# Turning the second batch's q by DMA instead of on the matrix engine, in a fused attention and feed-forward kernel

## The chip, the cores and the metric

The kernel runs on one core of a Trainium2 chip. The core has a matrix engine (TensorE, PE in the profile; its weight loads are shown as PEld), a vector engine (VectorE, DVE), an activation engine (ScalarE, ACT), a general engine (GpSimd, POOL) and a queue engine (SyncE, SP). Each works through its own list of instructions in order; semaphores tie the lists together. Transfers between the chip's memory and the core's SBUF are issued from SP, ACT or POOL, and carried out by 16 DMA engines. The metric is the device time of one execution in microseconds (us). Times in the trace count from the start of the span.

## The reference

Eight batches of eight heads go through a linear attention without softmax, are normalised per head, and then go through a gated feed-forward layer whose input is normalised per token:

```python
kv = np.einsum('bhsd,bhse->bhde', k, v)          # 64x64 per head
out = np.einsum('bhsd,bhde->bhse', q, kv)
out = out / sqrt(mean(out * out, -1) + 1e-6) * g_norm
x = out.transpose(0, 2, 1, 3).reshape(B * S, H * D)   # 4608 x 512
xn = x / sqrt(mean(x * x, -1) + 1e-6) * rms_g
out = (silu(xn @ w_gate) * (xn @ w_val)) @ w_out      # 512 -> 1536 -> 512
```

There are 576 tokens in a batch (S), 8 heads (H) of 64 (D). Inputs and output are float32; the kernel multiplies in bfloat16 and accumulates in float32.

## The kernel before, in words

**Tiles.** A batch's 576 tokens are cut into a main part of 512 (four chunks of 128, `NC = 4`) and a remainder of 64 (`REM`). The feed-forward layer works in nine groups of 512 tokens: group b is the main part of batch b, and the last group is the eight remainders together (`xr`). For a group, twelve pairs of products make the hidden tiles (`gate_of` with `wg`, `val_of` with `wv`, line 641), then 48 products with `wo` make four output tiles (line 676).

**q, k, v.** For `out = q kv` the matrix engine needs q with the head dimension on the partitions: that is `qTs`, the turned q, two buffers used by batch in turn. Three ways to get it stand in the program. Batch 0 casts q from a float32 stage and turns it on PE against an identity (`qT_mm`). Batches 2 to 7 load q as float32 on SP (`load_q`, line 217), cast it on POOL (batch 2: on ACT) into `main_q`, and turn it by a DMA on SP (`qT_dma`, lines 332 to 336):

```python
def qT_dma(self):
    flat = mains[self.b, 0].rearrange("p c h d -> p (c h d)")
    nc.sync.dma_start_transpose(out=self.qT[:, 0:NC].rearrange(...), in_=flat)
    rem = rems[0][self.b % 2][:REM].rearrange("p h d -> p (h d)")
    return nc.sync.dma_start_transpose(out=self.qT[:, NC, :, 0:REM], in_=rem)
```

Batch 1, the second, has a way of its own: a POOL-issued DMA loads q and casts it on the way to bfloat16, in the order heads, chunks, dimension (`load_cast`, line 187, into `qc`), and PE turns it head by head (`qT_heads`, line 314: 40 products of a 128 x 64 weight with the identity); DVE and ACT copy the results from PSUM into `qTs[1]` (`qT_out`, line 326).

**The order of the work.** The program writes each engine's list by hand. The feed-forward work is a row of slots; `Placer` keeps, for each slot, the small operations of attention that ride on it, and `emit` writes a slot's operations of other engines first, then the slot's own products, then its PE operations. The row that matters here starts when the second half (columns 256 to 511) of group 0 begins: slots 0 to 11 are that half's gate and value products (8 products of 256 columns each), slots 12 to 27 are the 48 products with `wo` of group 0, three to a slot (`slots_b_by_j`), and slot 28 is the first of group 1, which needs batch 1's turned and normalised result (`x`).

**Batch 1's steps** are put into fixed slots by `place_second(P, 9)` (line 588), all offsets counted from slot 9: `turn_q` on PE in slot 5, its copies in slots 6 to 8; the k-by-v products (`kv_mm`, line 273) in slot 9 and their copies in 10; `oT_mm` (line 380, the first reader of the turned q) in slots 11, 11, 12, 13, 14 for the four head pairs and the remainder; squares on ACT (`sqT_`) a slot or two behind; sums of squares (`stat_mm`) in 15; the output in token order (`o_mm`, line 341) in 16 to 19; the scale chain on DVE from 16; scaling in 18 to 22; and the turning of the result (`xT_mm`, line 520) in 20 to 25, with the last copies in 26.

**The queues around it.** POOL's list (lines 768 to 850) issues the loads of the weights, then waits for and casts batch 0's late q, then issues the cast loads of q, v and k of batch 1, the four loads of `w_out` (`load_wo`, line 230), and the k and v of batch 2. SP's list has, ahead of everything in the slots, `load_q(2)` (line 911: 1024 KB and 128 KB of float32 q of batch 2), which a hand-made dependency holds back until the first `w_out` load has landed. Behind it on SP come, in slot order, batch 2's `qT_dma` and the output stores.

Of the kernel before, what the change touches and what calls it, by code (L numbers as in the profile page):

```python
# [11 lines left out]
BF16 = mybir.dt.bfloat16  # L12
# [3 lines left out]
ACT = mybir.ActivationFunctionType  # L16
# [70 lines left out]
def kernel(  # L87
# [12 lines left out]
    nc = tc.nc  # L100
    B, H, S, D = q.shape
# [3 lines left out]
    NC = 4  # L105
    MAIN = 128 * NC
    REM = S - MAIN
    NS = d_model // 128
    NF = d_ff // 128
# [3 lines left out]
    OB = 3  # L113
# [7 lines left out]
    qkv = pool("qkv", 2)  # L121
# [9 lines left out]
    mm1_p = pool("mm1", 3, space=bass.MemoryType.PSUM)  # L131
    o2_p = pool("o2", 2, space=bass.MemoryType.PSUM)
    att_p = pool("att", 3, space=bass.MemoryType.PSUM)


    ident = consts.tile([128, 128], BF16, name="ident")
# [4 lines left out]
    vc, kc = ([consts.tile([128, H, (NC + 1) * D], BF16, name=f"{t}c{n}") for n in range(2)] for t in "vk")  # L141
    sel = consts.tile([128, 2, 2], BF16, name="sel")
    qc = consts.tile([128, H, (NC + 1) * D], BF16, name="qc1")
# [10 lines left out]
    qTs = [consts.tile([128, NC + 1, NS, 128], BF16, name=f"qTs{n}") for n in range(2)]  # L154
    rems = [[consts.tile([128, H, D], BF16, name=f"remq{n}") for n in range(2)]]
# [20 lines left out]
    mains, xs = {}, {}  # L176
# [10 lines left out]
    def load_cast(b, t, heads=None):  # L187
        to = qc if t == 0 else (vc if t == 2 else kc)[b % 2]
        if heads is None:
            return nc.gpsimd.dma_start(  # L190
                out=to[:REM, :, NC * D :], in_=src[t][b, :, MAIN:S, :].rearrange("h p d -> p h d")
            )
        view = src[t][b, :, 0:MAIN, :].rearrange("h (p c) d -> p h (c d)", c=NC)[:, heads[0] : heads[1]]
        return nc.gpsimd.dma_start(out=to[:, heads[0] : heads[1], : NC * D], in_=view)
# [27 lines left out]
    def loads_kv(b):  # L222
        return [lambda t=t, hs=hs: load_cast(b, t, hs) for t in (1, 2) for hs in ((0, H), None)]

    def load_w(n):
        cols = slice(FB0[n] * 128, (FB0[n] + FB[n]) * 128)
        first = nc.gpsimd.dma_start(out=wg[n], in_=moe_w_gate.rearrange("(s p) f -> p s f", p=128)[:, :, cols])
        return first, nc.gpsimd.dma_start(out=wv[n], in_=moe_w_val.rearrange("(s p) f -> p s f", p=128)[:, :, cols])

    def load_wo(n):  # L230
        view = moe_w_out.rearrange("(c p) d -> p c d", p=128)
        return nc.gpsimd.dma_start(out=wo[n], in_=view[:, n * OB : (n + 1) * OB, :])
# [9 lines left out]
    class Att:  # L242
        def __init__(self, b):
            self.b = b
            self.kv, self.qT = kvs[b % 2], qTs[b % 2]
            if b < 2:
                self.qTj = self.qT.rearrange("p c j t -> p (c j t)").rearrange("p (j c t) -> p j c t", j=NS, c=NC + 1)
            else:
                self.qTj = self.qT.rearrange("p c j t -> p j c t")
            self.kv_chunks = range(NC + 1)  # L250
            self.o, self.outa, self.sq = {}, {}, {}
            self.xT = {}
            self.st = None
# [50 lines left out]
        def qT_mm(self, js, chunks, pool=None):  # L304
            qT_ps = (pool or att_p).tile([128, len(js), len(chunks) * 128], BF16, name="o2" if pool else "att")
            for n, j in enumerate(js):
                for i, c in enumerate(chunks):
                    nc.tensor.matmul(
                        qT_ps[:, n, i * 128 : (i + 1) * 128], lhsT=self.pair(0, c, j), rhs=ident, is_transpose=True,
                        start=True, stop=True, skip_group_check=True,  # L310
                    )
            return qT_ps

        def qT_heads(self, js, chunks):
            qT_ps = att_p.tile([128, len(js), len(chunks) * 128], BF16, name="att")
            for n, j in enumerate(js):
                for i, c in enumerate(chunks):
                    for half in range(2):
                        nc.tensor.matmul(  # L319
                            qT_ps[half * D : (half + 1) * D, n, i * 128 : (i + 1) * 128],  # L320
                            lhsT=qc[:, 2 * j + half, c * D : (c + 1) * D], rhs=ident, is_transpose=True,
                            start=True, stop=True, skip_group_check=True,
                        )
            return qT_ps

        def qT_out(self, ps, js, c0, eng):
# [261 lines left out]
    def place_second(P, s):  # L588
        a = Att(1)
        V, A = nc.vector, nc.scalar  # L590
        ps = {}
        pe = lambda at, cost, n, fn: P.at("PE", cost, lambda: ps.__setitem__(n, fn()), s + at)
        dve = lambda at, cost, fn: P.at("DVE", cost, fn, s + at)
        act = lambda at, cost, fn: P.at("ACT", cost, fn, s + at)

        def turn_q():
            for n, (js, chunks) in enumerate(((P0, range(NC)), (P1, range(NC)), (ALL, (NC,)))):
                ps[n] = a.qT_heads(js, chunks)

        P.at("PE", 1.2, turn_q, s - 4)  # L600
        for j in range(2):
            dve(-3 + j, 0.42, lambda j=j: a.qT_out(ps[0][:, j : j + 1], (j,), 0, V))
            act(-3 + j, 0.58, lambda j=j: a.qT_out(ps[1][:, j : j + 1], (2 + j,), 0, A))
        act(-1, 0.58, lambda: a.qT_out(ps[2], ALL, NC, A))
        P.at("PE", 1.14, lambda: a.kv_mm(range(NS)), s)
        dve(1, 0.43, lambda: a.kv_half(0))
        dve(1, 0.43, lambda: a.kv_half(1))

        parts = [((j,), 0, NC) for j in range(NS)] + [(ALL, NC, NC + 1)]
        for n in range(NC + 1):  # L610
            pe((2, 2, 3, 4, 5)[n], 0.25, ("oT", n), lambda n=n: a.oT_mm(*parts[n]))
            act((3, 4, 4, 5, 6)[n], 0.62, lambda n=n: a.sqT_(ps["oT", n], *parts[n]))
        act(6, 1.28, lambda: A.preload_act_table(ACT.Sqrt))
        P.at("PE", 0.64, lambda: a.stat_mm(0, NC + 1), s + 6)
        for n in range(NC + 1):
            P.at("PE", 0.24, lambda n=n: a.o_mm(n, mm1_p if n == 2 else None), s + (7, 7, 8, 9, 10)[n])
        dve(7, 2.2, lambda: a.lead_chain(0, NC + 1, True))
        for c in range(NC + 1):
            dve(9 + c, 0.68, lambda c=c: a.xna_(c, V, a.o[c]))
        for at, js, cs in ((11, P0, (0, 1)), (13, P1, (0, 1)), (14, P0, (2, 3)), (15, P1, (2, 3))):  # L620
            P.at("PE", 0.24, lambda js=js, cs=cs: a.xT_mm(js, cs), s + at)
            for j in js:
                dve(at + 1, 0.3, lambda j=j, cs=cs: a.xT_out(j, cs, V))
        P.at("PE", 0.15, lambda: a.xT_mm(ALL, (NC,)), s + 16)
        dve(17, 0.62, lambda: [a.xT_out(j, (NC,), V) for j in ALL])
        P.floor = s + 18
        return s + 18

# [135 lines left out]
    V, G, A = nc.vector, nc.gpsimd, nc.scalar  # L764
    H0, H1 = (0, 4), (4, 8)
    P0, P1 = (0, 1), (2, 3)
    ALL = range(NS)
# [17 lines left out]
    make_identity(nc, ident)  # L785
    make_identity(nc, identf)
    w_loads = [load_w(n) for n in range(len(FB))]
    G.memset(rems[0][1][REM:], 0.0)
    G.memset(kvs[1], 0.0)
    for tile_ in (kc[0], kc[1], vc[0], vc[1], qc):  # L790
        G.memset(tile_[REM:, :, NC * D :], 0.0)

    def fold(w, s, eng):
# [6 lines left out]
    a = Att(0)  # L800
# [20 lines left out]
    for i, j in enumerate(P1):  # L821
        a.kv_pairs_out(kvb, i, j)
    V.tensor_scalar(
        out=gain, in0=gall[:, 0:NS], scalar1=gcol, scalar2=float(d_model) ** 0.5, op0=OP.mult, op1=OP.mult
# [20 lines left out]
    for t in (0, 2, 1):  # L845
        load_cast(1, t, (0, H))
        load_cast(1, t)
    wo_loads = [load_wo(n) for n in range(NF // OB)]
    for f in loads_kv(2):
        f()  # L850

    half = MAIN // 2
    early = [Slot("half", lambda: gates(0, range(FB[0]), 0, half))]
    for n, w in enumerate(FB):
        js = range(FB0[n], FB0[n] + w)
# [66 lines left out]
    P = Placer(slots, 3)  # L922
# [55 lines left out]
```

## Time and profile before

| | |
|---|---|
| median of 3 runs | 325.04 us (324.96 to 325.22) |
| the profiled execution | 324.99 us |
| its span in the trace | 323.2 us (1.8 us lie around it) |
| granted TensorE clock | 1.00 |
| PE busy | 312.9 us, 97% of the span |
| DVE, ACT, POOL busy | 178.7, 143.1, 89.3 us |
| DMA | 40.49 MB, a mean of 125 GB/s; 190 to 220 GB/s in the first 65 us |
| SP and ACT transfers (hardware queues) / POOL transfers (software queue) | 32.8% / 34.2% of 16 engines' span |

The page's first part gives each engine's busy time; the chain of work that ended last follows the program back from its last instruction, from each wait to what released it; the timeline lists one engine's instructions with the idle time before each and its releaser; the list of transfers gives, for each group of DMA issues, the size and the median time from issue to landing, and can be asked for a stretch of the span. A matmul's duration is a latency: starts of neighbours overlap, so what one costs is read from the distance of starts, or from the chain. On SP and POOL, a row for a DMA is the time the engine spends issuing it, not the transfer.

### The profile page before, as it was taken

To read this page: it belongs to the slowest core of one execution; us is meant where nothing else is said; L and a number is where in the kernel's file an instruction comes from. 1 tells how busy PE (TensorE), PEld (TensorE's weight loads), DVE (VectorE), ACT (ScalarE), POOL (GpSimd) and SP (SyncE) were. 2 spreads that over 40 slices of the span, in tenths; PEclk is the share of its full clock that TensorE was granted. 3 is DMA by queue.
4 is the path that set the end of the run, shared out by engine and by line. 5 is a ranking of instruction groups with operands and counts; after the bars stand their busy time and mean duration, and the time that the engine had idled before them with its cause. 6 is when DMAs were issued, how large, how long until landed. Compare 5 with 4: busy or idle time off the path is not lost.

```text
span 323.2 us, 5403 instructions
## 1 busy us (share of the span) xinstructions
PE 312.9 (97%) x2041; PEld 162.3 (50%) x2062; DVE 178.7 (55%) x394; ACT 143.1 (44%) x266; POOL 89.3 (28%) x110
## 2 busy tenths in 40 slices
PE   5999999999999999999999999999999999999995
PEld 1678866554454445444554445444544444444443
DVE  4658438489938672857185818681778133203411
ACT  1464566485758323832283228422742233223320
POOL 8763420049016600670067005800420000000000
PEclk9999999999999999999999999999999999999999
DMA  8999999949673984499559956896000800040002
GB/s 215 220 200 198 194 223 217 220 139 147 121 199 107 139 163 140 130 124 158 144 148 108 140 150 173 90 139 162 35 1 0 172 32 0 3 108 21 0 34 97
DMA packets 78213, 40.49 MB, mean 125 GB/s; under 512 B 41960, under 2 KB 73708, under 8 KB 78188
## 3 DMA queue, kind: packets, MB, share of 16 engines
q0 software_dynamic: 30672, 14.16, 34.2%
q1 hardware_dynamic: 46032, 25.01, 31.8%
q10 hardware_dynamic: 1484, 0.99, 1.0%
q8 instruction: 16, 0.26, 0.3%
q14 instruction: 9, 0.07, 0.1%
HBM read 37.78 MB, written 9.44 MB: 146 GB/s over the span
## 4 chain that ended last, share of the span: by engine, by line
PE 89%; DMA 5%; ACT 2%; issue 1%; DVE 1%; POOL 0%; SPq 0%; ACTq 0%; POOLq 0%
PE mm L641 55%; PE o L676 26%; DMA rstg<-in_q_dram 3%; DMA remv<-in_v_dram 2%; PE att L341 2%; PE att L273 2%; PE mm L676 1%; PE o L706 1%; ACT sq L367 0%; PE att L520 0%; ACT silu L650 0%; DVE h L659 0%; PE att L319 0%; ACT outa L371 0%; ACT wv L795 0%
## 5 line engine op out<-in xcount | busy, mean ns | idle before, releaser
L659 DVE TENSOR_TENSOR h<-silu,mm 128x512 bf16<-128x512 bf16 (+1 forms) x120 | 75.7, 631 | 82.4 <-PE mm L641 75.9
L650 ACT ACTIVATE silu<-mm 128x512 bf16<-128x512 f32 (+1 forms) x120 | 66.3, 556 | 82.5 <-PE mm L641 73.3
L641 PE MATMUL mm<-x,wv 128*128 128x512 bf16 (+1 forms) x431 | 99.8, 355 | 0.1
L641 PE MATMUL mm<-x,wg 128*128 128x512 bf16 (+1 forms) x419 | 98.5, 358 | 0.2 <-DVE h L659 0.2
L676 PE MATMUL o<-wo,h 128*128 128x512 bf16 x383 | 87.6, 379 | 1.3 <-issue 0.8
L422 POOL TENSOR_TENSOR sq<-sq,g 128x512 bf16<-128x512 bf16 x30 | 34.6, 1155 | 130.8 <-ACT sq L367 130.7
L641 PEld LDWEIGHTS <-wv 128*128 128x128 bf16 x480 | 46.2, 98 | 44.0
L641 PEld LDWEIGHTS <-wg 128*128 128x128 bf16 x468 | 44.7, 98 | 42.9 <-issue 0.6
L676 PEld LDWEIGHTS <-h 128*128 128x128 bf16 x420 | 40.2, 98 | 46.0 <-DVE h L659 0.2
L692 ACT COPY osb<-o 128x512 f32<-128x512 f32 x33 | 19.3, 587 | 69.4 <-PE o L676 69.4
L427 DVE TENSOR_REDUCE st<-sq 128x8 f32<-128x512 bf16 x60 | 38.8, 678 | 1.1 <-ACT sq L367 0.8
L302 DVE CAST kvs<-att 64x256 bf16<-64x256 f32 x14 | 5.9, 422 | 30.3 <-PE att L273 30.2
L367 ACT ACTIVATE sq<-att 128x512 bf16<-128x512 f32 x30 | 17.9, 598 | 2.2 <-PE att L341 2.2
L494 DVE TENSOR_TENSOR xna<-outa,al 128x512 bf16<-128x512 bf16 x30 | 18.7, 682 | 0.0
L371 ACT CAST outa<-att 128x512 bf16<-128x512 f32 x30 | 17.7, 590 | 0.0
L341 PEld LDWEIGHTS <-qTs 128*128 128x128 bf16 x140 | 10.2, 98 | 6.9
L641 PE MATMUL mm<-xr,wg 128*128 128x512 bf16 x47 | 12.3, 379 | 0.1
L641 PE MATMUL mm<-xr,wv 128*128 128x512 bf16 x47 | 12.3, 379 | 0.1
L341 PE MATMUL att<-kvs,qTs 128*128 128x128 bf16 x136 | 12.2, 219 | 0.0
L208 POOL CAST main_q<-stg 128x1024 bf16<-128x1024 f32 (+1 forms) x12 | 11.3, 976 | 0.7 <-DMA stg<-in_q_dram 0.7
L237 PE MATMUL mm<-idle 128*128 128x512 bf16 x26 | 7.5, 452 | 4.0 <-DVE idle L163 4.0
L795 ACT ACTIVATE wv<-wv,gain 128x384 bf16<-128x384 bf16 x16 | 9.2, 611 | 0.5 <-PE mm L641 0.5
(132 smaller groups left out, 174.5 us busy)
## 6 DMA issues: line engine op xcount, KB each, us to landing
out_dram<-osb SPq DMA_DIRECT2D x31, 256.0 KB, 2.6
stg<-in_q_dram SPq DMA_DIRECT2D x6, 1024.0 KB, 7.0
vc<-in_v_dram POOLq DMA_DIRECT2D x7, 512.0 KB, 8.3
kc<-in_k_dram POOLq DMA_DIRECT2D x7, 512.0 KB, 6.1
wg<-in_moe_w_gate_dram POOLq DMA_DIRECT2D x4, 384.0 KB, 15.6
wv<-in_moe_w_val_dram POOLq DMA_DIRECT2D x4, 384.0 KB, 16.8
wo<-in_moe_w_out_dram POOLq DMA_DIRECT2D x4, 384.0 KB, 13.2
out_dram<-osb SPq DMA_DIRECT2D x8, 128.0 KB, 2.3
```

Of the source, the lines that this page charges most:

```text
L208: return copy(out=mains[b, t][:, cs[0] : cs[1], h0:h1, :], in_=staged[b, t].rearrange("p h (c d) -> p c h d", c=NC)[:, cs[0] : cs[1], h0:h ...
L341: nc.tensor.matmul(o[:, 2 * j : 2 * j + 2, :], lhsT=self.qTj[:, j, c, :], rhs=self.kv[:, j, :, :], start=j == 0, stop=j == NS - 1, skip_gr ...
L367: nc.scalar.activation(out=self.sq[c][:, 0], in_=self.o[c], func=ACT.Square)
L371: (eng.tensor_copy if eng else nc.scalar.copy)(out=self.outa[c], in_=self.o[c])
L422: eng.tensor_tensor(out=self.sq[c][:, 1], in0=self.sq[c][:, 0], in1=g2, op=OP.mult)
L427: nc.vector.reduce_sum(out=self.st[:, which, c, :], in_=self.sq[c][:, which], axis=AX.X)
L494: return eng.tensor_tensor(out=self.xna[:, c], in0=src, in1=self.al[:, c, :].to_broadcast([128, H, D]), op=OP.mult)
L641: nc.tensor.matmul(ps[:, : c1 - c0], lhsT=w[n][:, s, jj * 128 : (jj + 1) * 128], rhs=x_of(g, s, c0, c1), start=s == 0, stop=s == NS - 1)
L650: nc.scalar.activation(out=sis[g, j][:, c0:c1], in_=ps, func=ACT.Silu)
L659: nc.vector.tensor_tensor(out=hs[g, j][:, c0:c1], in0=sis[g, j][:, c0:c1], in1=v_ps, op=OP.mult)
L676: nc.tensor.matmul(ps, lhsT=hs[g, j][:, t * 128 : (t + 1) * 128], rhs=wo[j // OB][:, j % OB, :], start=j == 0, stop=j == NF - 1)
L692: (eng.copy if eng is nc.scalar else eng.tensor_copy)(out=o, in_=ps)
```

## The change

Batch 1's q is still loaded by the POOL-issued cast DMA into `qc`, in the order of heads. POOL then copies it into the order of chunks: two copies (four heads each, 128 x 1024) into `mains[1, 0]` and one of the remainder (64 x 512) into `rems[0][1]`. They stand in POOL's list between the second and the third load of `w_out`. SP turns the result with the same `qT_dma` that the later batches use, placed in slot 5. `turn_q` with its 40 products on PE, and its five copies on DVE and ACT, are gone. All of batch 1's steps from `kv_mm` on stand one slot later; the slot in which later work may begin (`P.floor`, 27) is the same. `qTs[1]` takes the layout of the later batches, with chunks outermost, and one of POOL's early memsets is aimed at it, in place of two.

In SP's list the two transposes come directly behind `load_q(2)`. In PE's list batch 1's first `oT_mm` now stands behind the three products of slot 12.

```diff
@@ Att.__init__
-            if b < 2:
+            if b < 1:
                 self.qTj = self.qT.rearrange("p c j t -> p (c j t)").rearrange("p (j c t) -> p j c t", j=NS, c=NC + 1)
...
-        def qT_heads(self, js, chunks):
-            qT_ps = att_p.tile([128, len(js), len(chunks) * 128], BF16, name="att")
-            for n, j in enumerate(js):
-                for i, c in enumerate(chunks):
-                    for half in range(2):
-                        nc.tensor.matmul(
-                            qT_ps[half * D : (half + 1) * D, n, i * 128 : (i + 1) * 128],
-                            lhsT=qc[:, 2 * j + half, c * D : (c + 1) * D], rhs=ident, is_transpose=True,
-                            start=True, stop=True, skip_group_check=True,
-                        )
-            return qT_ps
...
@@ place_second
-        P.at("PE", 1.2, turn_q, s - 4)
-        for j in range(2):
-            dve(-3 + j, 0.42, lambda j=j: a.qT_out(ps[0][:, j : j + 1], (j,), 0, V))
-            act(-3 + j, 0.58, lambda j=j: a.qT_out(ps[1][:, j : j + 1], (2 + j,), 0, A))
-        act(-1, 0.58, lambda: a.qT_out(ps[2], ALL, NC, A))
-        P.at("PE", 1.14, lambda: a.kv_mm(range(NS)), s)
-        dve(1, 0.43, lambda: a.kv_half(0))
-        dve(1, 0.43, lambda: a.kv_half(1))
+        P.at("SP", 0.0, a.qT_dma, max(s - 4, 0))
+        P.at("PE", 1.14, lambda: a.kv_mm(range(NS)), s + 1)
+        dve(2, 0.43, lambda: a.kv_half(0))
+        dve(2, 0.43, lambda: a.kv_half(1))
...
-            pe((2, 2, 3, 4, 5)[n], 0.25, ("oT", n), lambda n=n: a.oT_mm(*parts[n]))
-            act((3, 4, 4, 5, 6)[n], 0.62, lambda n=n: a.sqT_(ps["oT", n], *parts[n]))
+            pe((3, 3, 4, 5, 6)[n], 0.25, ("oT", n), lambda n=n: a.oT_mm(*parts[n]))
+            act((4, 5, 5, 6, 7)[n], 0.62, lambda n=n: a.sqT_(ps["oT", n], *parts[n]))
...
@@ early memsets on POOL
-    G.memset(rems[0][1][REM:], 0.0)
+    G.memset(qTs[1][:, NC, :, REM:], 0.0)
     G.memset(kvs[1], 0.0)
-    for tile_ in (kc[0], kc[1], vc[0], vc[1], qc):
+    for tile_ in (kc[0], kc[1], vc[0], vc[1]):
...
@@ POOL's list behind the cast loads of batch 1
-    wo_loads = [load_wo(n) for n in range(NF // OB)]
+    wo_loads = [load_wo(n) for n in range(2)]
+    mains[1, 0] = qkv.tile([128, NC, H, D], BF16, name="main_q")
+    for h0, h1 in (H0, H1):
+        G.tensor_copy(
+            out=mains[1, 0][:, :, h0:h1, :], in_=qc[:, h0:h1, : NC * D].rearrange("p h (c d) -> p c h d", c=NC)
+        )
+    G.tensor_copy(out=rems[0][1][:REM], in_=qc[:REM, :, NC * D :])
+    wo_loads += [load_wo(n) for n in range(2, NF // OB)]
```

The lines left out move the remaining steps of `place_second` (the table load, `stat_mm`, `o_mm`, the scale chain, `xna_`, `xT_mm` and `xT_out`) from offset n to offset n + 1 in the same way.

More of the change, by code (lines that the diff above doesn't have):

```diff
@@ L594, in place_second @@
         act = lambda at, cost, fn: P.at("ACT", cost, fn, s + at)
-        def turn_q():
-            for n, (js, chunks) in enumerate(((P0, range(NC)), (P1, range(NC)), (ALL, (NC,)))):
-                ps[n] = a.qT_heads(js, chunks)
-        P.at("PE", 1.2, turn_q, s - 4)
-        for j in range(2):
-            dve(-3 + j, 0.42, lambda j=j: a.qT_out(ps[0][:, j : j + 1], (j,), 0, V))
-            act(-3 + j, 0.58, lambda j=j: a.qT_out(ps[1][:, j : j + 1], (2 + j,), 0, A))
-        act(-1, 0.58, lambda: a.qT_out(ps[2], ALL, NC, A))
-        P.at("PE", 1.14, lambda: a.kv_mm(range(NS)), s)
-        dve(1, 0.43, lambda: a.kv_half(0))
-        dve(1, 0.43, lambda: a.kv_half(1))
+        P.at("SP", 0.0, a.qT_dma, max(s - 4, 0))
+        P.at("PE", 1.14, lambda: a.kv_mm(range(NS)), s + 1)
+        dve(2, 0.43, lambda: a.kv_half(0))
+        dve(2, 0.43, lambda: a.kv_half(1))
         parts = [((j,), 0, NC) for j in range(NS)] + [(ALL, NC, NC + 1)]
         for n in range(NC + 1):
-            pe((2, 2, 3, 4, 5)[n], 0.25, ("oT", n), lambda n=n: a.oT_mm(*parts[n]))
-            act((3, 4, 4, 5, 6)[n], 0.62, lambda n=n: a.sqT_(ps["oT", n], *parts[n]))
-        act(6, 1.28, lambda: A.preload_act_table(ACT.Sqrt))
-        P.at("PE", 0.64, lambda: a.stat_mm(0, NC + 1), s + 6)
+            pe((3, 3, 4, 5, 6)[n], 0.25, ("oT", n), lambda n=n: a.oT_mm(*parts[n]))
+            act((4, 5, 5, 6, 7)[n], 0.62, lambda n=n: a.sqT_(ps["oT", n], *parts[n]))
+        act(7, 1.28, lambda: A.preload_act_table(ACT.Sqrt))
+        P.at("PE", 0.64, lambda: a.stat_mm(0, NC + 1), s + 7)
         for n in range(NC + 1):
-            P.at("PE", 0.24, lambda n=n: a.o_mm(n, mm1_p if n == 2 else None), s + (7, 7, 8, 9, 10)[n])
-        dve(7, 2.2, lambda: a.lead_chain(0, NC + 1, True))
+            P.at("PE", 0.24, lambda n=n: a.o_mm(n, mm1_p if n == 2 else None), s + (8, 8, 9, 10, 11)[n])
+        dve(8, 2.2, lambda: a.lead_chain(0, NC + 1, True))
         for c in range(NC + 1):
-            dve(9 + c, 0.68, lambda c=c: a.xna_(c, V, a.o[c]))
-        for at, js, cs in ((11, P0, (0, 1)), (13, P1, (0, 1)), (14, P0, (2, 3)), (15, P1, (2, 3))):
+            dve(10 + c, 0.68, lambda c=c: a.xna_(c, V, a.o[c]))
+        for at, js, cs in ((12, P0, (0, 1)), (14, P1, (0, 1)), (15, P0, (2, 3)), (16, P1, (2, 3))):
             P.at("PE", 0.24, lambda js=js, cs=cs: a.xT_mm(js, cs), s + at)
@@ L623, in place_second @@
                 dve(at + 1, 0.3, lambda j=j, cs=cs: a.xT_out(j, cs, V))
-        P.at("PE", 0.15, lambda: a.xT_mm(ALL, (NC,)), s + 16)
-        dve(17, 0.62, lambda: [a.xT_out(j, (NC,), V) for j in ALL])
+        P.at("PE", 0.15, lambda: a.xT_mm(ALL, (NC,)), s + 17)
+        dve(18, 0.62, lambda: [a.xT_out(j, (NC,), V) for j in ALL])
         P.floor = s + 18
```

## The prediction

> **What bounds the kernel now.** I read first the busy times, then the chain of work that ended last, in order of time, around batch 1's steps; each row of the chain is start, length and what ran.
>
> ```profile
> PE 312.9 (97%) x2041; PEld 162.3 (50%) x2062; DVE 178.7 (55%) x394; ACT 143.1 (44%) x266; POOL 89.3 (28%) x110
> ...
> 37.27 1.24 PE att L319 x40
> 38.50 3.60 PE mm L641 x32
> 42.10 0.81 PE att L273 x40
> 42.91 1.87 PE mm L641 x16
> 44.81 0.38 PE att L380
> 45.19 0.43 PE o L676 x2
> ```
>
> PE is the bound, and from 20 us on the chain is almost nothing but PE rows. So what leaves PE's list shortens the run, and what makes PE wait lengthens it by as much. The reader should see two places: the 40 products of line 319 are 1.24 us of the chain, and batch 1's first oT_mm (line 380) starts at 44.81 with no wait before it.
>
> Then SP's timeline, and the list of transfers asked for the stretches around 42.1, 42.5 and 55.1 us (the last figure is us from issue to landing); the first line is from the list of SP's waits (us in total, times, longest).
>
> ```profile
> SPq L183 <- DMA wo<-in_moe_w_out_dram: 13.0, 1, 13.0
> ...
> 42.09 0.37 SPq L183 DMA_DIRECT2D stg<-in_q_dram  x1
> 42.51 0.62 SPq L201 DMA_DIRECT2D rstg<-in_q_dram  x1
> 55.10 3.29 SPq L334 DMA_TRANSPOSE qTs<-main_q  x1
> 58.49 1.18 SPq L336 DMA_TRANSPOSE qTs<-remq  x1
> ...
> stg<-in_q_dram SPq DMA_DIRECT2D x1, 1024.0 KB, 11.0
> rstg<-in_q_dram SPq DMA_DIRECT2D x1, 128.0 KB, 12.6
> qTs<-main_q SPq DMA_TRANSPOSE x1, 5.2
> ```
>
> SP stands still until the first w_out load has landed and issues batch 2's q at 42.09; that is ahead of batch 1's new transposes in the same list. The 1024 KB land at 42.09 + 11.0 = 53.1, the 128 KB behind them at 42.51 + 12.6 = 55.1. Batch 2's own transposes, issued at 55.10, show the price of the operation: 5.2 us to landing, at 60.3.
>
> Last, POOL's timeline where the copies go in, POOL's groups with the shapes kept apart, and PE's spinning products at the start, in three stretches (count: duration ns min/median/max, first and last start us).
>
> ```profile
> 30.71 0.76 POOL L232 DMA_DIRECT2D wo<-in_moe_w_out_dram  x1 [1.19 <-DMA wv<-in_moe_w_val_dram]
> 33.63 0.76 POOL L232 DMA_DIRECT2D wo<-in_moe_w_out_dram  x1 [2.16 <-DMA qc<-in_q_dram]
> 40.20 0.89 POOL L194 DMA_DIRECT2D vc<-in_v_dram  x1 [1.78 <-PE mm L641]
> ...
> L208 POOL CAST main_q<-stg 128x1024 bf16<-128x1024 f32 x10 | 10.1, 1048 | 0.0
> L215 POOL CAST remq<-rstg 64x512 bf16<-64x512 f32 x6 | 3.7, 612 | 1.6 <-DMA rstg<-in_q_dram 1.6
> ...
> L237 PE MATMUL mm<-idle x4: 634/634/634, 4.4 to 5.7; 128*128 128x512 bf16 x4
> L237 PE MATMUL mm<-idle x6: 379/380/634, 6.5 to 7.9; 128*128 128x512 bf16 x6
> L237 PE MATMUL mm<-idle x7: 379/379/379, 8.8 to 10.1; 128*128 128x512 bf16 x7
> ```
>
> **What is removed.** The 40 products: 1.24 us of PE, all on the chain: -1.24. The five copies (two on DVE at 0.42 us, three on ACT at 0.58 us, between 37.9 and 40.8) stand where both engines wait for PE between two operations (DVE idles 1.29 us before its product at 39.59): 0. One memset fewer on POOL, some 0.5 us at about 16 us, where POOL waits 0.65 us for batch 0's q anyway: 0.
>
> **POOL's copies.** Two of 128 x 1024 and one of 64 x 512, by the rows of the same shapes from float32: 2 x 1.05 + 0.61 = 2.7 us. They need qc, which landed by 33.6 (POOL's third w_out load waited for exactly that), so they end at about 36.3. The source is bfloat16 here; half or twice the row would move that by -1.4 or +2.7 us, and since SP comes to the transposes only at 43.1, both change nothing. Queued behind them on POOL are the third and fourth w_out loads (33.6 and 34.6 become 36.3 and 37.1) and batch 2's k; the v load behind those waits for PE until 40.20, with 1.78 us of idle time, and takes up the rest. Those two w_out loads landed 12.2 and 14.2 us after issue, so they come at 48.5 and 51.3; their first readers are slots 20 and 24, which ran at 52.5 and 55.7 before, and 1.24 us earlier if PE never waits: 0, with 2.7 us to spare.
>
> **SP's transposes.** SP is free of load_q(2) at 42.51 + 0.62 = 43.13, and issues them then. The data is in place, so what counts is when the main one lands. Low end: it overtakes the load, 43.1 + 4.4 (the fastest landing of the six such transposes) = 47.5. High end: the slowest landing, 8.6, counted only from the load's landing at 55.1: 63.7. In between are the rows I take: the 128 KB behind the 1024 KB landed 2.0 us after them although it had been issued 0.4 us later, and no row of the queue shows a small transfer passing a large one. So the transposes move when the load is through, at about 55.1, just where batch 2's transposes moved before, beside the same rest of batch 2's k and v loads. Those needed until 60.3 from an issue at 55.1; of that I take off 1.2 us, in which no data moved yet (batch 3's were issued at 79.83, and the DMA engines' share is 0.17 in the microsecond from 80 and 1.03 in the one from 81), since here the issue lies long before: 59.1.
>
> **The new wait on PE.** The first oT_mm needs the main transpose. PE's work up to the end of slot 11 is unchanged but for the 1.24 us, and now the three products of slot 12 (0.65 us, since two take 0.43 in the chain) come before it: PE is there at 44.81 - 1.24 + 0.65 = 44.2. It waits until 59.1: 14.9 us. Queued behind it on PE is all that follows, the 45 other products of slots 13 to 27 included, though their weights and hidden tiles are ready; ACT's squares and DVE's chain wait for PE. The remainder's transpose, 1.2 to 2.7 us behind by its issue and landing rows, is read three slots later: 0. Batch 2's q, landed at 53.1, waits for ACT to come to its cast in slot 19; before, ACT waited 1.2 us for it there, so relative to PE nothing becomes later. The step of one slot in the later parts costs 0.6 us of margin at slot 28: its last copy of x ended at 57.4 and PE came at 58.7: 0.
>
> **A cold start after the wait.** The spinning products begin 0.43 us apart after PE's idle start (1.3 us for three intervals) and end 0.215 apart, the change lying near 7 us: 3 us at half speed, 1.5 us lost. After 14.9 us of idling I take the same, 1.5; the low end is 0 (a pause of 0.49 us at 15.8 left no trace), the high end twice the row, 3.
>
> The rule on this, in the Trainium skill, TensorE: Matmul & The Clock Gate, section "What's actually happening": after an idle window of about 3.4 us the array runs at half clock, until a window of about 3.4 us of steady work has passed. The trace's start agrees, with 3 us. By that figure the cost would be 1.7 and the sum 0.2 higher; without any such effect it would be 1.5 lower.
>
> **Sum**, against the profiled execution's 324.99 (which stands 0.05 under the median, so nothing is added): -1.24 + 14.9 + 1.5 = +15.2, **340.1 us**, 4.6% slower.
>
> **The rivals.**
>
> *The transposes pass the load.* If they ran beside the load, they would land between 47.5 and 51.7 (43.1 + 8.6). PE waits 3.3 to 7.5 us: with -1.24 and 0 to 1.5 for the cold start, 327.1 to 332.8. For it: no row has a transpose behind a load, so their order is inferred. Against: the 128 KB row above. The Trainium skill, DMA: Bandwidth & Descriptors, section "Queues, rings and completion order", has each engine take descriptors in ring order, but says too that completion isn't in order of issue; the first speaks against this rival, and no run here shows the second.
>
> *Partly through.* The load gets through sooner than before, or some of the 16 engines are done with it early, and the transposes land at 52 to 57: 333 to 338. For it only that 2.0 us lie between the load's two landings, so its end is not sharp; against it that the same bytes are under way on POOL's queue.
>
> *Worse contention.* The transposes crawl beside batch 2's k and v (landing until 58.3) as in the slowest row, up to 63.7: at 61 the time is 342, at 63.7 it is 344.7.
>
> *The other side: the wait does not form.* The first w_out load would have to land so early that load_q(2) and the transposes are through at 44.2; it decides at an issue about 1 + 4.4 us sooner, at 39 or before, and with the transposes past the load. Then -1.24: 323.8. For it only that POOL's pause keeps two loads out of the queue from 33.6 to 36.3; against it, that these stand behind the first w_out load in any case, and that its landing at 42.0 is set by what is ahead of it.
>
> **How the numbers follow.** The forecast (transposes behind the load, landing at 57 to 61, 338 to 342) 0.66; partly through 0.10; passing the load 0.12; worse contention 0.09; no wait 0.03. The range must leave out no more than 0.2: from 333 (all of the passing case and no wait are left out, 0.15) to 344 (some 0.02 of the crawling one). A difference under 0.2% (0.65 us) can't be told from none in this kernel. Faster 0.03, same 0.01, slower 0.96.
>
> **What would show it.** In the new profile: no row for line 319's products; the POOL copies between 33.6 and 36.5; SP's transposes issued near 43 with a landing of 14 to 17 us; a PE wait of about 15 us before batch 1's oT_mm, released by the DMA into qTs; products 0.43 us apart for about 3 us behind it; and from there on the old pattern, shifted. The forecast is wrong if the transposes land in 5 to 9 us, if SP issues them well before 42, or if the engines' pattern behind slot 28 isn't the old one.

## The result, and the profile after

The changed kernel takes 343.44 us (median of four runs, 342.98 to 343.75), the kernel before 325.00 (four runs, 324.87 to 325.22). The ratio is 1.0556, 95% interval 1.0541 to 1.0571. The profiled execution after took 343.33 us with a span of 341.5; 1.8 us lie around it, as before, so the 18.3 us between the two spans are the whole difference.

The changed kernel's page: busy times, the slices of the granted clock, the hardware queue that SP uses (packets, MB, share), and the group with the longest new idle time on PE. In the changed file `oT_mm` is line 368, the transposes are lines 322 and 324, and POOL's copies lines 831 and 834.

```profile
PE 315.0 (92%) x2022; PEld 161.6 (47%) x2022; DVE 177.4 (52%) x392; ACT 141.5 (41%) x263; POOL 91.2 (27%) x112
...
PEclk9999985699999999999999999999999999999999
...
q1 hardware_dynamic: 48400, 25.60, 31.4%
...
L368 PE MATMUL att<-qTs,kvs 128*128 128x512 bf16 (+1 forms) x8 | 2.4, 389 | 18.1 <-DMA qTs<-main_q 18.1
```

PE is busy 2.1 us longer than before (315.0 against 312.9), although 40 products are gone, and it idles 18.1 us in one piece, until the main transpose has landed. The clock row shows a dent there. The hardware queue has 2,368 packets and 0.59 MB more than before (46,032 and 25.01): the two new transposes, at 250 bytes a packet.

The chain that ended last, around that place:

```profile
43.64 18.32 DMA qTs<-main_q
...
62.09 1.01 PE att L368 x2
```

SP's timeline, then the list of transfers for the stretch from 43.1 to 48 us (the last figure is us from issue to landing):

```profile
42.50 0.37 SPq L183 DMA_DIRECT2D stg<-in_q_dram  x1
42.92 0.63 SPq L201 DMA_DIRECT2D rstg<-in_q_dram  x1
43.64 11.54 SPq L322 DMA_TRANSPOSE qTs<-main_q  x1
```

```profile
rstg<-in_q_dram SPq DMA_DIRECT2D x1, 128.0 KB, 12.4
qTs<-main_q SPq DMA_TRANSPOSE x1, 18.3
```

The load ahead ends at 42.92 + 12.4 = 55.3, the main transpose at 43.64 + 18.3 = 61.96, which is 6.6 us behind it. SP itself was held for 11.54 us by issuing that one transpose.

PE's timeline at the end of the wait and at slot 28, then slot 28 in the kernel before, and the granted clock in the stretches around the wait (PE busy, PEld, DVE, ACT, POOL, clock, DMA share, GB/s):

```profile
62.09 1.01 PE L368 MATMUL att<-qTs,kvs 128*128 128x512 bf16 x2 [18.07 <-DMA qTs<-main_q]
...
77.14 1.03 PE L621 MATMUL mm<-x,wg 128*128 128x512 bf16 x4
```

```profile
58.67 1.03 PE L641 MATMUL mm<-x,wg 128*128 128x512 bf16 x4
```

```profile
48.00:49.00 1.00, 0.00 (x0) 0.00 (x0) 0.00 (x0) 0.00 (x0) 0.00 (x0) 0.67 1.22 257
62.00:65.00 3.00, 2.90 (x7) 1.05 (x8) 0.00 (x0) 1.23 (x3) 0.00 (x0) 0.50 0.00 0
65.00:66.00 1.00, 1.00 (x5) 0.45 (x4) 0.00 (x0) 0.45 (x1) 0.00 (x0) 0.80 0.00 0
```

The way from the first oT_mm to slot 28 takes 77.14 - 62.09 = 15.05 us; before it took 58.67 - 44.81 = 13.86, of which 0.65 were the products that now come ahead. That is 1.84 us more. The clock is at 0.50 until about 65.4: its mean of 0.80 from 65 to 66 is 0.4 us at 0.50 and the rest at 1.00, and from 66 on it reads 1.00. Behind slot 28 both kernels need the same: 323.2 - 58.67 = 264.5 before and 341.5 - 77.14 = 264.4 after.

### The profile page after: what moved, and what is told of

Same layout as the page of the kernel before. It is cut to its first block, busy times and chain, and to the rows that moved or that the text cites. A ratio compares the mean times of both kernels' runs of the same rounds, so it can differ in the third digit from the quotient of the medians.

```text
span 341.5 us, 5346 instructions
## 1 busy us (share of the span) xinstructions
PE 315.0 (92%) x2022; PEld 161.6 (47%) x2022; DVE 177.4 (52%) x392; ACT 141.5 (41%) x263; POOL 91.2 (27%) x112
## 4 chain that ended last, share of the span: by engine, by line
PE 81%; DMA 17%; issue 0%; SPq 0%; POOL 0%; DVE 0%; POOLq 0%
PE mm L621 49%; PE o L656 25%; DMA qTs<-main_q 5%; DMA wg<-in_moe_w_gate_dram 5%; DMA wo<-in_moe_w_out_dram 4%; DMA vc<-in_v_dram 2%; PE att L329 2%; PE mm L656 2%; PE att L273 1%; PE o L686 1%; PE att L368 1%; PE att L508 0%; POOL remv L748 0%; PE mm L686 0%; SPq L201 0%
## 5 line engine op out<-in xcount | busy, mean ns | idle before, releaser
L656 PE MATMUL o<-wo,h 128*128 128x512 bf16 x396 | 90.5, 380 | 0.0
L368 PE MATMUL att<-qTs,kvs 128*128 128x512 bf16 (+1 forms) x8 | 2.4, 389 | 18.1 <-DMA qTs<-main_q 18.1
L359 ACT CAST outa<-att 128x512 bf16<-128x512 f32 x30 | 17.7, 591 | 0.0
L379 ACT ACTIVATE sqT<-att 128x512 bf16<-128x512 f32 x5 | 2.9, 596 | 21.3 <-PE att L368 21.3
## 6 DMA issues: line engine op xcount, KB each, us to landing
wo<-in_moe_w_out_dram POOLq DMA_DIRECT2D x4, 384.0 KB, 12.7
```

The source lines that it names most:

```text
L359: (eng.tensor_copy if eng else nc.scalar.copy)(out=self.outa[c], in_=self.o[c])
L656: nc.tensor.matmul(ps, lhsT=hs[g, j][:, t * 128 : (t + 1) * 128], rhs=wo[j // OB][:, j % OB, :], start=j == 0, stop=j == NF - 1)
```

## The experiments

The theory to begin with was the prediction's: the main transpose lands late because it stands in SP's queue behind batch 2's q. The first rival was that transposes are slow in this stretch wherever they stand, because POOL's loads share the DMA engines with them.

**The transposes ahead of the load in SP's list.**

```diff
-        P.at("SP", 0.0, a.qT_dma, max(s - 4, 0))
...
+    Att(1).qT_dma()
     gate = load_q(2)
```

> The changed kernel with one thing undone: in SP's list batch 1's two transposes stand ahead of batch 2's q load, not behind it. Theory (the wait on PE comes from the place behind the load): POOL's copies end at 36.8 and SP issues then; the main transpose lands 5 to 9 us later, at 42 to 46, against 61.96 before, PE waits 0 to 2 us instead of 18.1, no half clock, and the time falls from 343.4 to between 323.5 and 327. Rival (the transposes are slow in themselves beside POOL's loads, wherever they stand): they still need about 18 us, land near 55, PE waits about 11 us, and the time is near 336.

Measured: 335.0 us (333.98 to 336.03), ratio to the kernel before 1.029 (1.026 to 1.032). SP's timeline:

```profile
35.59 7.80 SPq L322 DMA_TRANSPOSE qTs<-main_q  x1
...
45.21 0.69 SPq L183 DMA_DIRECT2D stg<-in_q_dram  x1
```

The transpose lands 17.7 us after its issue, at 53.3, with nothing ahead of it in its queue, and PE still waits 9.2 us. The rival's number (336) is met and the theory's (323.5 to 327) missed by 8 us: the place behind the load is worth 8.4 of the 18.4 us, and not the whole. Those 8 us are the earlier issue (35.59 in place of 43.64); from issue to landing the transpose takes nearly as long as in the changed kernel, 17.7 against 18.3. What takes the rest is seen when the list of DMA queues is asked for the two microseconds from 40 to 42 of this run (packets, MB, share of 16 engines):

```profile
q0 software_dynamic: 312, 0.31, 90.9%
q1 hardware_dynamic: 302, 0.08, 29.8%
```

POOL's queue (q0) and SP's (q1) move the same number of packets, but POOL's are of 1 KB and those of the transpose of 256 bytes. So the transpose gets a quarter of the bytes of its neighbour. The main one, 512 KB, has 2,048 such packets; at 151 a microsecond they need 13.6 us, and the first of them moved only some 4 us after the issue (last section). This was the new theory: the two queues take turns, packet for packet. The Trainium skill, DMA: Bandwidth & Descriptors, section "Queues, rings and completion order", has each engine go round the queues and change at packet boundaries; the counts here agree.

**The load in another queue at the same time.** Batch 2's q is issued by ACT in slot 11, the transposes are held until the same moment (the first w_out load landed):

```diff
+            tc.add_manual_dep(t0.ins, wo_loads[0].ins.name, SYNC, reason="as the load")
...
+        P.at("ACT", 0.0, load_two, s + 2)
...
-    gate = load_q(2)
```

> The changed kernel with batch 2's q load issued from ACT's queue, just when SP issued it, and the transposes on SP held back until the same moment (the first w_out load landed, 42.4). So both are under way together in two queues, with the same bytes. Theory (order within SP's queue): the main transpose lands 6 to 9 us after its issue, at 49 to 51; PE waits 5 to 7 us; 330 to 333. Rival (the engines are shared, whichever the queue): it lands at 58 to 62 and the time stays at 340 to 344.

Measured: 340.11 us (339.87 to 340.51), ratio 1.045 (1.043 to 1.046). The main transpose was issued at 42.07 and landed after 15.9 us, at 58.0; PE waited 13.9 us. That is near the rival's case, at the early end of its ranges. The queues from 48 to 50 us:

```profile
q0 software_dynamic: 287, 0.15, 53.5%
q10 hardware_dynamic: 290, 0.30, 41.7%
q1 hardware_dynamic: 289, 0.07, 28.0%
```

With three queues at work each has a third of the packets. Out of the load's queue the transpose gains little: it lands 15.9 us after its issue in place of 18.3. It gets one turn in three from about 46 us on, in place of one in two from about 54, when the load ahead of it is through.

**Batch 2's v held back until the transposes have landed.**

```diff
+            done = a.qT_dma()
+            for f in loads_kv(2)[2:]:
+                tc.add_manual_dep(f().ins, done.ins.name, SYNC, reason="v of batch 2 later")
```

> The changed kernel with batch 2's v load on POOL held back until the transposes have landed; in the changed kernel it landed at 60.4 to 61.6, beside them. Theory (my price for the main transpose, 4.0 us behind the load, was too low by 2.9 because the transposes share the engines with that load): it lands at 58.5 to 59.5 instead of 61.96, and the time falls by 2.5 to 3.5, to 340 to 341. Rival (the transposes take 6.7 us behind the load by themselves): 61 to 62, and 342.5 to 343.5.

Measured: 338.91 us (338.38 to 340.2), ratio 1.042 (1.039 to 1.045). The transpose, issued at 43.33, lands after 14.1 us at 57.5, 4.5 us earlier than in the changed kernel, and the median falls by 4.5. That is earlier than the theory had it, and further from the rival: sharing with that load was worth 4.5 us, not 2.9. The queue of SP alone, from 56 to 58 us of this run, and both queues of the changed kernel in the same stretch:

```profile
q1 hardware_dynamic: 1074, 0.26, 58.7%
```

```profile
q0 software_dynamic: 476, 0.24, 87.8%
q1 hardware_dynamic: 478, 0.12, 46.3%
```

In the kernel before, batch 2's own transposes, issued at 55.10, met less of POOL's traffic. Its queues from 54 to 56 us, and from 58 to 60:

```profile
q0 software_dynamic: 830, 0.38, 145.2%
q1 hardware_dynamic: 42, 0.01, 4.2%
```

```profile
q1 hardware_dynamic: 1740, 0.44, 101.8%
```

There POOL's queue had the two microseconds from 54 nearly to itself and moved 830 packets; in the changed kernel it moved 424 in the same stretch, because batch 1's transposes, waiting behind the load, took turns with it (427 packets) as soon as the load was through.

**POOL's later loads held back too.** Here the transposes stand first on SP, as in the first experiment, and the third and fourth w_out loads and batch 2's k and v wait for them:

```diff
+    turned = Att(1).qT_dma()
+    late = load_wo(2)
+    tc.add_manual_dep(late.ins, turned.ins.name, SYNC, reason="the turned q first")
+    wo_loads += [late, load_wo(3)]
     for f in loads_kv(2):
```

> The run with the transposes first in SP's list, and besides POOL's third and fourth w_out loads and batch 2's k and v held back until both transposes have landed. New theory (packets of the two queues take turns one for one, so the transposes, 2048 packets of 256 bytes, move at some 155 a us beside POOL's 1 KB packets and at 566 a us alone, as in the run with v held back): about 780 go beside the second w_out load until it lands near 45, the rest in 2.2 us, landing near 48 instead of 53.4; PE waits 4 to 5 us; 328 to 330. Rival (a transpose needs some 18 us in this stretch whatever runs beside it): landing at 52 to 54 and 333 to 336.

Measured: 329.99 us (329.51 to 330.66), ratio 1.015 (1.014 to 1.017). The transpose lands at 35.35 + 12.7 = 48.05, PE waits 3.7 us, and the time is at the upper end of what the new theory gave. The wait is shorter than the 4 to 5 us of that theory; the time is not, because the cold start behind it cost more than in the changed kernel (see the next part). The queues from 44 to 46 us, when POOL had nothing more to move:

```profile
q1 hardware_dynamic: 1434, 0.36, 123.0%
q0 software_dynamic: 11, 0.01, 2.8%
```

Alone, SP's queue moves 717 packets in a microsecond, 4.7 times what it moved beside POOL's 1 KB packets. By then nearly all packets of both transposes were through; the landing came 2 us later, which the new theory had not counted.

**The same bytes in few packets.** With the transposes first on SP, the main one is replaced by a plain copy, so that batch 1's main q is moved and not turned:

```diff
+            if self.b == 1:
+                nc.sync.dma_start(out=self.qT[:, 0:NC].rearrange("p c j t -> p (c j t)"), in_=flat)
```

> The run with the transposes first in SP's list, with the main transpose of batch 1 replaced by a plain copy of the same 512 KB in rows of 4 KB (batch 1's main q is then not turned, which is left out of the computation; the transpose of the remainder stays). New theory (the number of packets sets the landing, not the bytes): the copy has a few hundred packets or fewer and lands 5 to 7 us after its issue at 35.6, by 43; PE doesn't wait, or under 1 us for the first w_out load; 323.5 to 325.5. Rival (bytes or a fixed delay in this stretch): it lands near 50 and the time is 330 or more.

Measured: 324.62 us (324.11 to 325.04), ratio 0.9982 (0.9973 to 0.9991). The copy lands 6.9 us after its issue at 35.82, at 42.7, and PE waits only 0.21 us, for the first w_out load. The queues from 40 to 42 us, the stretch shown for the first experiment:

```profile
q1 hardware_dynamic: 142, 0.47, 63.7%
q0 software_dynamic: 150, 0.15, 43.0%
```

Again one packet for one, but the copy's are of some 3.3 KB and bring 0.47 MB where the transpose brought 0.08. So it is the number of packets, not of bytes, that made the transpose late here. The copy differs from the transpose in kind too; against turning as such being slow stands the run before, where SP's queue, nearly all of it transposes, moved 717 packets in a microsecond once nothing ran beside it. The run also bounds the idea: with a turned q that came in time, the 1.24 us taken from PE would have been worth some 0.2% of the time (0.5 to 0.6 us). In the profiled execution, the fastest of ten with 324.11 us, PE reached the first oT_mm at 44.48, 0.98 us earlier than before with the products of slot 12 counted, which is the 1.24 less the wait of 0.21 to within 0.05; slot 28 came at 57.91, 0.76 earlier.

**Products in the wait.** 78 products on idle data stand ahead of batch 1's first oT_mm in the changed kernel:

```diff
-lambda n=n: a.oT_mm(*parts[n]))
+lambda n=n: a.oT_mm(*parts[n], None, 78 * (n == 0)))
```

> The changed kernel with 78 products on idle data ahead of batch 1's first oT_mm, about 16.9 us of PE's 18.1 us of waiting, so that PE is never idle for more than about 1.5 us. Theory (the pause also costs a cold start: the granted clock was 0.50 from 49 to 65): the stretch from the end of the wait to slot 28 shrinks from 15.05 to 13.2 us and the time falls by 1.8, to 341.6. Rival (that stretch is longer for another reason, ACT or DVE restarting behind PE): it stays at 15.05 and the time at 343.4.

Measured: 341.16 us (341.11 to 341.42), ratio 1.048 (1.046 to 1.050). PE's timeline:

```profile
43.91 17.00 PE L237 MATMUL att<-idle 128*128 128x512 bf16 x78
61.60 0.59 PE L368 MATMUL att<-qTs,kvs 128*128 128x512 bf16 x2 [0.69 <-DMA qTs<-main_q]
75.02 1.03 PE L621 MATMUL mm<-x,wg 128*128 128x512 bf16 x4
```

The way to slot 28 is 75.02 - 61.60 = 13.42 us against 15.05, 1.6 less, at a clock of 1.00 throughout. The profiled executions lie 2.16 us apart (343.33 and 341.17); nearly all of the rest is the landing, 0.4 earlier in this one. The cold start is real and costs 1.6 us here.

It does not cost the same in every run. Measured against these 13.42, the way from the first oT_mm to slot 28 is 1.3 us longer with v held back (14.69), 2.6 longer with the transposes first (15.98), 2.8 with the load on ACT (16.23) and 2.9 with POOL's loads held back (16.28), though PE's pause was only 3.7 us there. The clock stayed at 0.50 for 2.6, 5.2, 5.7 and 5.8 us after the restart, and half of each is the loss. Why that time differs was not tried.

**The two remaining parts, each alone in the kernel before.** First the steps from `kv_mm` on one slot later:

```diff
-        P.at("PE", 1.14, lambda: a.kv_mm(range(NS)), s)
+        P.at("PE", 1.14, lambda: a.kv_mm(range(NS)), s + 1)
...
```

> The kernel before, with only the steps of batch 1 from the k-by-v products on placed one slot later; q is still turned on PE. Theory (margin of 0.6 us at slot 28, priced at nothing): 325.0 within 0.6 us. Rival (the later steps push slot 28 back): up to 0.9 us slower.

Measured: 325.11 us (median of 11 runs), ratio 1.0000 (0.9991 to 1.0008). Then POOL's copies, read by nobody:

```diff
-    wo_loads = [load_wo(n) for n in range(NF // OB)]
+    wo_loads = [load_wo(n) for n in range(2)]
...
+    wo_loads += [load_wo(n) for n in range(2, NF // OB)]
```

> The kernel before, with POOL's three copies between the second and third w_out load, read by nobody; q is still turned on PE. Theory (2.7 us of POOL, with the w_out loads 2.7 us later and no reader waiting, priced at nothing): 325.0 within 0.6 us. Rival (a late w_out load holds PE): 0.7 to 2.7 us slower, with a PE wait on w_out at slot 20 or 24.

Measured: 325.02 us (median of 11 runs), ratio 0.9998 (0.9989 to 1.0007). Neither part changes the time by anything that can be measured.

No run that turns the whole of batch 1's q by DMA is faster than the kernel before: the nearest, with POOL's loads held back, is 1.5% slower.

## Why the prediction was right, and where it was not

The direction, the place and the form were right, and 343.4 lies inside the range, near its upper end of 344; the point of 340.1 was 3.3 us too low. The forecast case itself (338 to 342, at 0.66) was missed. The result lies inside the range only because the range took in most of the rival of worse contention, so that part of the agreement is luck.

- *What is removed, -1.24 us.* PE came to the wait at 44.0 where 44.2 was forecast. The copies and the memset cost nothing.
- *POOL's copies, 0.* They ran from 34.19 to 36.8 and took 2.6 us, as priced; alone they change nothing.
- *One step later, 0.* Shown by the run with that alone.
- *SP's transposes, landing at 59.1.* This is the step that failed. They were issued at 43.64, as forecast, but landed at 61.96, outside even the 57 to 61 of the forecast case. The term "5.2 - 1.2", 4.0 us behind the load, measured 6.6. I took batch 2's own transposes as the row for it and held the neighbours, "the same rest of batch 2's k and v loads", to be equal. They weren't: in the kernel before, POOL's queue was empty by 58.3, and from 58 to 60 us SP's queue moved 1,740 packets with none of POOL's beside them; in the changed kernel v's loads ran until 61.6, and the packets took turns until about 60. The 1.2 us taken off, in which no data moved yet, belonged to a gap of nearly 2 us (54.5 to 56.4) in which SP's queue moved next to nothing and POOL's could get ahead; with the transposes waiting in the queue this gap was gone, and POOL's loads were slowed as well. Holding v back moved the landing by 4.5 us.
- *The reason behind that step.* "So the transposes move when the load is through" holds for the changed kernel, but I took the place behind the load to be what makes them late. Undone, it gives back 8.4 of the 18.4 us, by the earlier issue. What no step had is the price of 2,048 small packets beside a busy queue, and the two queues' counts of packets, which show it, could have been asked of the trace of before: from 48 to 50 us it has 334 packets for each queue.
- *The new wait, 14.9 us.* 18.07, which is 3.2 more: 2.9 by the later landing, 0.2 because PE was at the wait earlier, and 0.1 between landing and start.
- *The cold start, 1.5 us.* 1.84 by the stretch to slot 28, of which 1.6 vanish when PE is kept busy. The other 0.2 is not the clock: the two runs with the steps one slot later and no pause to speak of (the plain copy, and the step alone) need 13.43 for that stretch too, against 13.21 before. The clock fell 4.3 us after PE had stopped at 44.0 (the mean of 0.67 from 48 to 49 puts the change at about 48.3) and came back 3.3 us after it had restarted at 62.1. That the size came out so near is in part luck, since the same cost lay between 1.3 and 2.9 us in the other runs. The Trainium skill, TensorE: Matmul & The Clock Gate, section "What's actually happening", gives the array its full clock after about 3.4 us of sustained work; the 3.3 here agrees, and the estimate of 1.7 from that figure was as near as the row of the first products, but the other runs' 2.6 to 5.8 us differ from it.
- *Sum.* -1.24 + 18.07 + 1.84 = 18.67, less 0.2 by which PE was earlier at the wait and 0.15 less behind slot 28, is the measured 18.3.
- *The rivals.* The transposes did not pass the load, and the wait did form. "Worse contention" was nearest, and for the right reason: its 61 to 63.7 holds the measured landing. It deserved more than 0.09.

## What to carry to other kernels

In these runs a transfer's price beside another busy queue went by its number of packets, not by its bytes: before a DMA transpose goes into a stretch where another queue is busy, count its packets and the packets that the other queue moves per microsecond there. A transpose that is hidden in one stage (5.2 us here) can take 18 us in another, and moving it up in its own queue or to another queue cures only part of that. And a wait of several microseconds on the matrix engine has to be priced with the cold start behind it, which was between 1.3 and 2.9 us here.

## What the runs showed of the hardware that I had not expected

- Queues whose packets were all on the move moved nearly equal counts of them: 312 and 302, 287 and 290 and 289, 142 and 150 in two microseconds, whatever their sizes of 256 bytes to over 3 KB. With a third queue (ACT's) at work, each had a third of the packets.
- Behind POOL's backlog SP's first packets moved late: transposes issued at 35.59 show no packet from 36 to 38 us, 13 from 38 to 40 and 302 from 40 to 42. Batch 3's in the kernel before, with little else under way, began about 1.2 us after issue. Why the backlog delays a queue that had nothing ahead of it was not tried, and stays open.
- Issuing a DMA transpose held SP for 2.0 to 5.2 us in the kernel before, 7.8 in the first experiment and 11.54 in the changed kernel, where the load stood ahead of it. What comes behind it on SP waits for that too.
